# Reordering the side jobs of a decode layer's backward pass, with two small loads moved to the sync queue

## The chip, the cores and the metric

The kernel runs on one core of a Trainium2 chip. The time is device microseconds (us) of one execution; the median of three runs of the kernel before is 818.56 us, the runs lie between 818.16 and 818.86. One execution was profiled; what is read from its profile is set against that execution's own time, 818.39 us.

The core has five engines that run their own instruction streams in order: PE (matmul; its weight loads are listed as PEld), DVE (vector), ACT (scalar), POOL (GpSimd) and SP (sync). SP and POOL are used here above all to issue DMAs. The core's 16 DMA engines move the bytes.

## The reference

One decode step (one token, width D = 448) of a layer, forward and backward. In short:

```
h   = x  + Attention(layernorm(x))        # 16 query heads, 8 key/value heads, head width 256
h2  = h  + FFN(layernorm(h))              # (n @ w_gate) * (n @ w_up) @ w_down, width 1792
```

Attention looks only at the last W = 4096 of the 32768 cached positions. The outputs are h2 and the gradients of a loss with respect to x, k_cache, v_cache, wq, wo, w_gate, w_up and w_down, given grad_out, all in bf16. The two cache gradients have the caches' full shape, 8 x 32768 x 256 each: they are zero except in the window. Of these zeros 16 pieces (8 heads, two tensors) of 14.3 MB each have to be written, 234.9 MB in all. The nonzero windows are another 16 pieces of 2 MB.

## The kernel before

**Two DMA queues.** `FILL` is the sync queue (SP issues), `IO` the GpSimd queue (POOL issues). The sync queue carries only the 16 zero fills (L58), from one tile `zeros` of 128 x 8192 that DVE clears at the very start (L54). They are independent of all else. At most eight are outstanding: the ninth waits for the first to land, and so on. Everything else goes through the GpSimd queue in program order: inputs, windows of K and V, weights, and all other outputs.

**Start.** POOL first issues the two 0.9 KB rows x and grad_out (L88, L90), then Wq (L92, 3.5 MB), K and V windows (L75) and w_down (L97). Each row is needed by DVE for the first layernorm, after the clearing of `zeros`.

**Forward.** For each of the eight heads g: `scores`, `softmax`, `moments` (L266 to L329). Then wo (L376), the second layernorm, w_gate and w_up, and the gradients through the FFN (L423) to dh (L432), doT (L435), dq (L453 to L460).

**Backward.** A loop over g = 0..7 (stages). Each stage has 64 transposes of a V window on PE (L554), copied out of PSUM by ACT and DVE in turn (`evac`, L210 and L212); products dp (L559); some small work on DVE (L565 to L576); 32 matmuls `d_ps` (L588) whose results ACT and DVE copy to a staging slot; and two DMAs of 2 MB each to the cache gradients (L593). V windows of heads 5 to 7 are loaded again into slots that stages 1 to 3 have freed.

**Side jobs.** After each stage the list `side[g]` is run. Its jobs are
- `outer` (L472 to L477): one or two outer products' worth of rows of a weight gradient, made on DVE (L476) in one of two staging buffers in `Mt`, and one DMA on the GpSimd queue (L477). A buffer is free again when its DMA has landed. o6, o7: w_gate, w_up; o5: wo; o8: w_down; o4: wq.
- `ffn_out` (L490 to L501): loads w_down a second time into `Rt` (L492), 14 + 28 matmuls (L497, L159), and writes h2.
- `dxn_part` (L507 to L511): loads a part of Wq a second time into `Rt` (L508; 4 of 7 blocks, then 3), and reduces it against dq on DVE (L510).
- `dx_out`: the backward of the first layernorm (L194 to L203) and the output dx (L519).

`Rt` is one tile: w_up and the row `bc2[1]` that the o7 jobs read lie in it, then w_down, then the parts of Wq, so these follow each other. A scheduler orders the instructions of each engine; it moves ready work ahead of the program's order, so a job need not run where the program text has it.

Of the kernel before, what the change touches and what calls it, by code (L numbers as in the profile page):

```python
# [7 lines left out]
bf16 = mybir.dt.bfloat16  # L8
# [5 lines left out]
D = 448  # L14
# [14 lines left out]
HQ = H * Dh // 2  # L29
HF = F // 2  # L30
# [10 lines left out]
def kernel(  # L41
# [4 lines left out]
    FILL = nc.sync  # L46
    IO = nc.gpsimd

    const = ctx.enter_context(tc.tile_pool(name="const", bufs=1))
    small = ctx.enter_context(tc.tile_pool(name="small", bufs=2))  # L50
    ps = ctx.enter_context(tc.tile_pool(name="ps", bufs=1, space=bass.MemoryType.PSUM))

    zeros = const.tile([128, ZW], bf16)
    V_.memset(zeros[:], 0.0)  # L54
    for g in range(G):
# [27 lines left out]
    def flat_rows(w):  # L83
        return w.rearrange("a b -> (a b)").rearrange("(p x) -> p x", p=128)


    x_bf = const.tile([1, D], bf16, tag="rowa", name="x_bf")
    IO.dma_start(out=x_bf[:], in_=A_x.rearrange("a b d -> (a b) d"))  # L88
    go_bf = const.tile([1, D], bf16, tag="rowb", name="go_bf")
    IO.dma_start(out=go_bf[:], in_=grad_out.rearrange("a b d -> (a b) d"))  # L90
    wq_sb = S[:, 1:3, :].rearrange("p a b -> p (a b)")[:, 0:NI * HQ]
    IO.dma_start(out=wq_sb, in_=flat_rows(A_wq))  # L92
    load_K(0)
# [58 lines left out]
    def half_to_row(dst, z, bcast, first=True):  # L152

        d3 = dst.rearrange("o (m r) -> o m r", r=NI)
        n = 0
        for i in range(NI):
            for s in range(2):
                lt = z[:, i:i + 1].to_broadcast([128, 128]) if bcast else z[:, i:i + 1]
                P_.matmul(d3[:, :, (7 * s + i) // 2], lhsT=lt, rhs=ident_f[:, s::2],  # L159
                          start=(first and n == 0), stop=(n == 2 * NI - 1), skip_group_check=True)  # L160
                n += 1
# [6 lines left out]
    def layernorm(X, tag):  # L168
        s1 = small.tile([128, 1], f32, tag="ln_s")
        V_.reduce_sum(out=s1[:], in_=X, axis=AX)  # L170
        nm = small.tile([128, 1], f32, tag="ln_nm")
        V_.tensor_scalar(out=nm[:], in0=total(s1[:], 1)[:], scalar1=-1.0 / (2 * D), scalar2=None, op0=ALU.mult)
        xc = small.tile([128, NI], f32, tag="ln_xc")
        V_.tensor_scalar(out=xc[:], in0=X, scalar1=nm[:, 0:1], scalar2=None, op0=ALU.add)
        sq = small.tile([128, NI], f32, tag="ln_sq")
        s2 = small.tile([128, 1], f32, tag="ln_s2")
        V_.tensor_tensor_reduce(out=sq[:], in0=xc[:], in1=xc[:], scale=1.0, scalar=0.0, op0=ALU.mult, op1=ALU.add, accum_out=s2[:])
        rstd = const.tile([128, 1], f32, tag=tag + "rstd")
        S_.activation(out=rstd[:], in_=total(s2[:], 1)[:], func=ACT.Sqrt, bias=eps_t[:, 0:1], scale=1.0 / (2 * D))
        V_.reciprocal(out=rstd[:], in_=rstd[:])  # L180
        xh = const.tile([128, NI], f32, tag=tag + "xh")
        V_.tensor_scalar(out=xh[:], in0=xc[:], scalar1=rstd[:, 0:1], scalar2=None, op0=ALU.mult)
        xb = const.tile([128, NI], bf16, tag=tag + "xb")
        V_.tensor_copy(out=xb[:], in_=xh[:])
        xf = const.tile([128, NI], f32, tag=tag + "xf")
        V_.tensor_copy(out=xf[:], in_=xb[:])
        xx = const.tile([128, NI, 2], bf16, tag=tag + "xx")
        V_.tensor_tensor(out=xx[:], in0=xf[:].unsqueeze(2).to_broadcast([128, NI, 2]), in1=msk[:], op=ALU.mult)
        return rstd, xh, xf, xx
# [30 lines left out]
    rstd1, xh1, xf1, xx1 = layernorm(xX[:], "ln1")  # L220
# [21 lines left out]
    oT_f = const.tile([128, 32], f32)  # L242
    oT_bf = const.tile([128, 32], bf16)
    kbar = const.tile([128, 32], f32)
    dh2_bc = const.tile([128, D], bf16)
# [96 lines left out]
    bc2 = [S[:, 7, NI * HF:NI * HF + F].rearrange("p (i c) -> p i c", i=2), Rt[:, NI * HF:NI * HF + F].rearrange("p (i c) -> p i c", i=2)]  # L342
# [43 lines left out]
    rstd2, xh2, xf2, xx2 = layernorm(hX[:], "ln2")  # L386
# [44 lines left out]
    dh_bc = const.tile([128, D], bf16)  # L431
# [30 lines left out]
    dq_bc = late[:, 0:2 * HQ].rearrange("p (i c) -> p i c", i=2)  # L462
# [4 lines left out]
    def stage_buf():  # L467
        k = 1 + st_ctr[0] % 2
        st_ctr[0] += 1
        return late[:, k * 4096:(k + 1) * 4096]  # L470

    def outer(dst, n0, n1, src, scal, width):  # L472

        sb = stage_buf()[:, 0:(n1 - n0) * width].rearrange("p (n c) -> p n c", c=width)
        for n in range(n0, n1):
            V_.tensor_scalar(out=sb[:, n - n0, :], in0=src(n), scalar1=scal[:, n:n + 1], scalar2=None, op0=ALU.mult)  # L476
        IO.dma_start(out=dst[:, n0:n1, :], in_=sb)  # L477

    o4 = flat_rows(out_4).rearrange("p (i c) -> p i c", i=NI)
    o5 = out_5.rearrange("(b p) n -> p b n", p=128)  # L480
    o6 = flat_rows(out_6).rearrange("p (i c) -> p i c", i=NI)
    o7 = flat_rows(out_7).rearrange("p (i c) -> p i c", i=NI)
    o8 = out_8.rearrange("(c p) n -> p c n", p=128)

    hh = const.tile([128, FC], f32)
# [4 lines left out]
    def ffn_out():  # L490
        wd1 = Rt[:, 0:FC * D].rearrange("p (c n) -> p c n", n=D)
        IO.dma_start(out=wd1, in_=B_w_down.rearrange("(c p) n -> p c n", p=128))  # L492
        hX2 = small.tile([128, NI], f32, tag="hX2")
        V_.tensor_scalar(out=hX2[:], in0=hX[:], scalar1=0.5, scalar2=None, op0=ALU.mult)
        t = ps.tile([1, D], f32, tag="tmp", bufs=1)
        for c in range(FC):
            P_.matmul(t[:], lhsT=hh_bf[:, c:c + 1], rhs=wd1[:, c, :], start=(c == 0), stop=False, skip_group_check=True)  # L497
        half_to_row(t[:], hX2[:], False, first=False)
        h2 = const.tile([1, D], bf16, tag="rowb", name="h2")
        V_.tensor_copy(out=h2[:], in_=t[:])  # L500
        IO.dma_start(out=out_0.rearrange("a b d -> (a b) d"), in_=h2[:])  # L501

    Pq = const.tile([128, NI], f32)
    wq2 = Rt[:, 0:4 * HQ].rearrange("p (i c) -> p i c", c=HQ)
    wq_d = flat_rows(A_wq).rearrange("p (i c) -> p i c", i=NI)

    def dxn_part(i0, i1):  # L507
        IO.dma_start(out=wq2[:, 0:i1 - i0, :], in_=wq_d[:, i0:i1, :])  # L508
        for i in range(i0, i1):
            V_.tensor_tensor_reduce(out=wq2[:, i - i0, :], in0=wq2[:, i - i0, :], in1=dq_bc[:, i % 2, :], scale=1.0, scalar=0.0,  # L510
                                    op0=ALU.mult, op1=ALU.add, accum_out=Pq[:, i:i + 1])  # L511

    def dx_out():
# [4 lines left out]
        V_.tensor_copy(out=dx[:], in_=t[:])  # L518
        IO.dma_start(out=out_1.rearrange("a b d -> (a b) d"), in_=dx[:])  # L519

    side = {
        0: [lambda: outer(o6, 0, 4, lambda i: bc2[0][:, i % 2, :], xf2, HF), lambda: outer(o6, 4, 7, lambda i: bc2[0][:, i % 2, :], xf2, HF),
            lambda: outer(o7, 0, 4, lambda i: bc2[1][:, i % 2, :], xf2, HF), lambda: outer(o7, 4, 7, lambda i: bc2[1][:, i % 2, :], xf2, HF)],
        1: [ffn_out] + [lambda b=b: outer(o5, b, b + 8, lambda n: dh_bc[:], oT_f, D) for b in (0, 8)],
        2: [lambda b=b: outer(o5, b, b + 8, lambda n: dh_bc[:], oT_f, D) for b in (16, 24)],
        3: [lambda b=b: outer(o8, b, b + 7, lambda n: dh2_bc[:], hh, D) for b in (0, 7)],
        4: [lambda: dxn_part(0, 4)],
        5: [lambda: dxn_part(4, 7), dx_out],
        6: [lambda i=i: outer(o4, i, min(i + 2, 7), lambda n: dq_bc[:, n % 2, :], xf1, HQ) for i in (0, 2)],
        7: [lambda i=i: outer(o4, i, min(i + 2, 7), lambda n: dq_bc[:, n % 2, :], xf1, HQ) for i in (4, 6)],  # L530
    }


    STG = [5, 6, 7, 0]
# [3 lines left out]
    rowb = late[:, 14336:16384].rearrange("p (k a c) -> p k a c", k=2, a=8)  # L538
# [7 lines left out]
    for g in range(G):  # L546
# [36 lines left out]
        for c in range(T // 2):  # L583
            d_ps = bps.tile([128, 2, 2, Dh], f32, tag="d2", bufs=2)
            for i in range(2):
                t = 2 * c + i
                k, a = t // 8, t % 8
# [38 lines left out]
```

## Time and profile before

| What | Value |
|---|---|
| Median of three runs | 818.56 us |
| The profiled execution: time / span of its instructions | 818.39 / 816.6 us |
| PE, DVE, ACT, POOL busy | 61%, 46%, 20%, 5% of the span |
| Bytes moved by DMA | 338.66 MB: 234.88 MB on the sync queue, 103.00 MB on the GpSimd queue, the rest instruction loads |
| Mean DMA rate over the span | 415 GB/s |
| Granted PE clock | 0.85 to 0.91 of full in the first 200 us, 0.50 to 0.53 from 400 us on |

How to read it: the profile divides the span into slices and gives for each engine the busy share, for the DMA engines the mean busy share of all 16 and the bytes moved. A stretch in which all 16 are busy reads 1.00 or 1.01. A wait is listed with the instruction that waited, what released it, the total in us, how often, and the longest one. For a DMA the time from its issue to its landing is given.

### The profile page before, as it was taken

How to read it: one execution, taken by the hardware profiler on the slowest of the kernel's cores; microseconds unless marked ns; L12 is line 12 of the kernel's file. 1: busy time of each engine (PE TensorE's matmuls, PEld its weight loads, DVE VectorE, ACT ScalarE, POOL GpSimd, SP SyncE). 2: the span in 40 equal slices, each digit the busy share in tenths (PEclk: the TensorE clock that was granted, in tenths of full speed). 3: DMA queues.
4: the chain of work that ended last, by engine and by line, in shares of the span. 5: the costliest groups of instructions: out<-in, count | busy, mean ns of one | idle time of the engine just before them, and what ended most of it. 6: DMA issues, size and time to landing. Idle time of an engine off the chain costs nothing.

```text
span 816.6 us, 12117 instructions
## 1 busy us (share of the span) xinstructions
PE 497.6 (61%) x4947; PEld 300.9 (37%) x4991; DVE 376.8 (46%) x1149; ACT 164.9 (20%) x261; POOL 41.7 (5%) x77
## 2 busy tenths in 40 slices
PE   3558869999574946062993468799378940001770
PEld 3545646666343523031981332345124410001110
DVE  4127847667461643028732354565255440404550
ACT  0220201221101000000011233355244420000440
POOL 4000000000000001000000000010010000000000
PEclk9959888999695969565555556555555555555555
DMA  8999999999999999999999999999999999999985
GB/s 322 431 424 429 427 429 426 429 427 426 432 423 426 424 420 418 427 429 432 423 430 427 417 413 426 428 402 429 419 404 426 423 428 400 424 415 432 431 355 237
DMA packets 24632, 338.66 MB, mean 415 GB/s; under 512 B 1312, under 2 KB 1376, under 8 KB 4736
## 3 DMA queue, kind: packets, MB, share of 16 engines
q1 hardware_dynamic: 14592, 234.88, 68.2%
q0 software_dynamic: 9984, 103.00, 30.2%
q8 instruction: 39, 0.64, 0.3%
q14 instruction: 17, 0.14, 0.0%
HBM read 57.28 MB, written 280.59 MB: 414 GB/s over the span
## 4 chain that ended last, share of the span: by engine, by line
issue 50%; DMA 22%; PE 14%; another core or an unknown queue 4%; DVE 4%; POOL 2%; ACT 1%; POOLq 0%; DVEq 0%; ACTq 0%
DMA out_dram<-Mt 9%; DMA out_dram<-S 5%; DMA S<-in_A_wo_dram 4%; PE dq_ps L453 3%; PE d_ps L588 3%; PE tr L554 2%; DMA S<-in_A_v_cache_dram 2%; DMA S<-in_A_wq_dram 2%; PE MT L322 2%; DVE Rt L423 1%; DVE Rt L510 1%; POOL S L75 1%; PE dh_ps L159 1%; DVE S L212 1%
## 5 line engine op out<-in xcount | busy, mean ns | idle before, releaser
L322 PE MATMUL MT<-Rt,S 128*128 128x512 bf16 x468 | 146.7, 391 | 22.5 <-DMA S<-in_A_v_cache_dram 19.8
L588 PE MATMUL d_ps<-R,Mt 32*128 32x512 bf16 x256 | 121.1, 605 | 58.6 <-DVE S L212 57.9
L318 DVE TENSOR_SCALAR Rt<-S,pf 128x256 bf16<-128x256 bf16 x512 | 118.0, 282 | 31.6 <-PE acc L329 16.5
L212 DVE CAST S<-d_ps 128x512 bf16<-128x512 f32 x128 | 87.1, 689 | 63.4 <-ACT S L210 55.6
L210 ACT CAST S<-d_ps 128x512 bf16<-128x512 f32 x128 | 74.9, 586 | 127.7 <-PE d_ps L588 127.7
L266 PE MATMUL tr<-ident_bf,S 128*128 128x128 bf16 x512 | 51.5, 264 | 43.4 <-DMA S<-in_A_k_cache_dram 40.1
L325 PEld LDWEIGHTS <-S 128*128 128x128 bf16 x512 | 50.1, 99 | 62.9 <-issue 7.2
L554 PE MATMUL tr<-ident_bf,S 128*128 128x128 bf16 x512 | 67.6, 304 | 0.7 <-ACT Mt L210 0.7
L588 PEld LDWEIGHTS <-Mt 32*128 32x128 bf16 x256 | 22.8, 113 | 112.8 <-issue 110.8
L329 PE MATMUL acc<-ones_bf,Rt 128*128 128x1 bf16 x1024 | 62.0, 164 | 0.0
L554 PEld LDWEIGHTS <-S 128*128 128x128 bf16 x512 | 48.4, 136 | 24.4 <-issue 24.4
L266 PEld LDWEIGHTS <-S 128*128 128x128 bf16 x512 | 40.5, 120 | 41.9 <-DMA S<-in_A_k_cache_dram 40.6
L325 PE MATMUL acc<-pT_all,S 128*128 128x2 bf16 x512 | 49.3, 166 | 2.6 <-issue 0.9
L165 PE MATMUL t<-st,ones_f 128*128 128x2 f32 x4 | 1.2, 364 | 79.6 <-DVE st L196 79.6
L210 ACT COPY Rt<-tr 128x1024 bf16<-128x1024 bf16 x32 | 32.4, 1012 | 85.1 <-PE tr L266 84.6
L210 ACT COPY Mt<-tr 128x1024 bf16<-128x1024 bf16 x32 | 32.4, 1014 | 60.8 <-PE tr L554 34.3
L329 PEld LDWEIGHTS <-Rt 128*128 128x128 bf16 x1024 | 44.5, 96 | 0.0
L212 DVE COPY Rt<-tr 128x1024 bf16<-128x1024 bf16 x32 | 22.1, 689 | 47.5 <-PE tr L266 46.2
L322 PEld LDWEIGHTS <-S 128*128 128x128 bf16 x512 | 32.2, 97 | 22.3 <-DMA S<-in_A_v_cache_dram 20.0
L331 ACT COPY Mt<-MT 128x512 f32<-128x512 f32 x8 | 4.7, 586 | 165.1 <-remote 73.8
L510 DVE CUSTOM_DVE_ANT_0 Rt<-Rt,Mt 128x2048 bf16<-128x2048 bf16 x7 | 15.6, 2289 | 48.3 <-DMA Rt<-in_A_wq_dram 48.3
L212 DVE COPY Mt<-tr 128x1024 bf16<-128x1024 bf16 x32 | 22.0, 686 | 22.9 <-PE tr L554 15.5
(184 smaller groups left out, 463.5 us busy)
## 6 DMA issues: line engine op xcount, KB each, us to landing
out_dram<-zeros SPq DMA_DIRECT2D x16, 14336.0 KB, 155.7
out_dram<-S POOLq DMA_DIRECT2D x16, 2048.0 KB, 31.0
S<-in_A_v_cache_dram POOLq DMA_DIRECT2D x11, 2048.0 KB, 35.6
S<-in_A_k_cache_dram POOLq DMA_DIRECT2D x8, 2048.0 KB, 27.9
out_dram<-Mt POOLq DMA_DIRECT2D x6, 896.0 KB, 18.2
S<-in_A_wq_dram POOLq DMA_DIRECT2D x1, 3584.0 KB, 15.3
S<-in_A_wo_dram POOLq DMA_DIRECT2D x2, 1792.0 KB, 35.6
out_dram<-Mt POOLq DMA_DIRECT2D x3, 1024.0 KB, 32.5
```

The lines of the kernel that those rows point to most:

```text
L75: IO.dma_start(out=dst, in_=cache[0, g, Sk - W:, :].rearrange("(p t) d -> p t d", t=T))
L210: S_.copy(out=out, in_=in_)
L212: V_.tensor_copy(out=out, in_=in_)
L266: P_.transpose(tr[:, i, dh, :], Xw[:, 4 * q + i, dh * 128:(dh + 1) * 128], ident_bf[:])
L318: V_.tensor_scalar(out=pk[:, i, h, :], in0=K[:, t, :], scalar1=pf[:, t, h:h + 1], scalar2=None, op0=ALU.mult)
L322: P_.matmul(MT[:, hf, :], lhsT=Vv[:, t, hf * 128:(hf + 1) * 128], rhs=pk[:, i, :, :].rearrange("p h d -> p (h d)"), start=(t == 0), stop=( ...
L325: P_.matmul(acc[:, 2 * hf:2 * hf + 2], lhsT=Vv[:, t, hf * 128:(hf + 1) * 128], rhs=pT_all[:, g, t, :], start=(t == 0 and hf == 0), stop=(t ...
L329: P_.matmul(acc[:, 4 + 2 * h + dk:5 + 2 * h + dk], lhsT=pk[:, i, h, dk * 128:(dk + 1) * 128], rhs=ones_bf[:, 0:1], start=False, stop=(t == ...
L453: P_.matmul(dq_ps[:, 2 * h + dk:2 * h + dk + 1], lhsT=Mt[:, h // 2, hf, c0:c0 + 128], rhs=doT_f[:, 2 * h + hf:2 * h + hf + 1], start=(hf = ...
L510: V_.tensor_tensor_reduce(out=wq2[:, i - i0, :], in0=wq2[:, i - i0, :], in1=dq_bc[:, i % 2, :], scale=1.0, scalar=0.0, op0=ALU.mult, op1=A ...
L554: P_.transpose(tr[:, i, dh, :], Vw[g][:, 4 * q + i, dh * 128:(dh + 1) * 128], ident_bf[:])
L588: P_.matmul(d_ps[:, i, :, :].rearrange("p w d -> p (w d)"), lhsT=rows[32 * k:32 * k + 32, a, :], rhs=R[32 * k:32 * k + 32, :], start=True, ...
```

## The change

The loads of x and grad_out are issued first of all by SP on the sync queue, ahead of the fills. `dxn_part` no longer loads; a new `dxn_load` does. The second load of w_down with `ffn_out`, the two o7 jobs, and the load of the first part of Wq stand ahead of the stage loop. The first reduction and the second load of Wq come with stage 0, the second reduction and dx with stage 1; o5, o8 and o4 follow in stages 2 to 6, and stage 7 has no side job.

```diff
+    x_bf = const.tile([1, D], bf16, tag="rowa", name="x_bf")
+    FILL.dma_start(out=x_bf[:], in_=A_x.rearrange("a b d -> (a b) d"))
+    go_bf = const.tile([1, D], bf16, tag="rowb", name="go_bf")
+    FILL.dma_start(out=go_bf[:], in_=grad_out.rearrange("a b d -> (a b) d"))
     zeros = const.tile([128, ZW], bf16)
     V_.memset(zeros[:], 0.0)
...
-    x_bf = const.tile([1, D], bf16, tag="rowa", name="x_bf")
-    IO.dma_start(out=x_bf[:], in_=A_x.rearrange("a b d -> (a b) d"))
-    go_bf = const.tile([1, D], bf16, tag="rowb", name="go_bf")
-    IO.dma_start(out=go_bf[:], in_=grad_out.rearrange("a b d -> (a b) d"))
     wq_sb = S[:, 1:3, :].rearrange("p a b -> p (a b)")[:, 0:NI * HQ]
...
+    def dxn_load(i0, i1):
+        IO.dma_start(out=wq2[:, 0:i1 - i0, :], in_=wq_d[:, i0:i1, :])
+
     def dxn_part(i0, i1):
-        IO.dma_start(out=wq2[:, 0:i1 - i0, :], in_=wq_d[:, i0:i1, :])
         for i in range(i0, i1):
...
     side = {
-        0: [o6 rows 0-4, o6 rows 4-7, o7 rows 0-4, o7 rows 4-7],
-        1: [ffn_out, o5 rows 0-8, o5 rows 8-16],
-        2: [o5 rows 16-24, o5 rows 24-32],
-        3: [o8 rows 0-7, o8 rows 7-14],
-        4: [lambda: dxn_part(0, 4)],
-        5: [lambda: dxn_part(4, 7), dx_out],
-        6: [o4 rows 0-2, o4 rows 2-4],
-        7: [o4 rows 4-6, o4 row 6],
+        0: [o67_job(0, 0, 4), o67_job(0, 4, 7), lambda: dxn_part(0, 4), lambda: dxn_load(4, 7)],
+        1: [lambda: dxn_part(4, 7), dx_out],
+        2: [o5_job(0), o5_job(8)],
+        3: [o5_job(16), o5_job(24)],
+        4: [lambda b=b: outer(o8, b, b + 7, lambda n: dh2_bc[:], hh, D) for b in (0, 7)],
+        5: [o4_job(0), o4_job(2)],
+        6: [o4_job(4), o4_job(6)],
+        7: [],
     }
+    ffn_out()
+    o67_job(1, 0, 4)()
+    o67_job(1, 4, 7)()
+    dxn_load(0, 4)
```

(The removed lists of jobs are written out in words here; `o4_job`, `o5_job` and `o67_job` are the same calls of `outer` as before under a name.) In the changed program POOL issues, from the end of the FFN's backward on: w_down, two outputs of weight gradients, h2, one output, Wq blocks 0 to 3, two outputs, the V window, Wq blocks 4 to 6, and only then the two windows of stage 0.

More of the change, by code (lines that the diff above doesn't have):

```diff
@@ L519, in dx_out, with o4_job, o5_job, o67_job @@
         IO.dma_start(out=out_1.rearrange("a b d -> (a b) d"), in_=dx[:])
-    side = {
[L522 to L526, printed above, removed]
-        4: [lambda: dxn_part(0, 4)],
-        5: [lambda: dxn_part(4, 7), dx_out],
-        6: [lambda i=i: outer(o4, i, min(i + 2, 7), lambda n: dq_bc[:, n % 2, :], xf1, HQ) for i in (0, 2)],
-        7: [lambda i=i: outer(o4, i, min(i + 2, 7), lambda n: dq_bc[:, n % 2, :], xf1, HQ) for i in (4, 6)],
-    }
+    def o4_job(i):
+        return lambda: outer(o4, i, min(i + 2, 7), lambda n: dq_bc[:, n % 2, :], xf1, HQ)
+    def o5_job(b):
+        return lambda: outer(o5, b, b + 8, lambda n: dh_bc[:], oT_f, D)
+    def o67_job(w, i0, i1):
+        return lambda: outer((o6, o7)[w], i0, i1, lambda i: bc2[w][:, i % 2, :], xf2, HF)
+    side = {
+        0: [o67_job(0, 0, 4), o67_job(0, 4, 7), lambda: dxn_part(0, 4), lambda: dxn_load(4, 7)],
[6 more added lines that the diff above has]
+        7: [],
+    }
+    ffn_out()
+    o67_job(1, 0, 4)()
+    o67_job(1, 4, 7)()
+    dxn_load(0, 4)
     STG = [5, 6, 7, 0]
```

## The prediction

> **What bounds the kernel now.** I read the page's slices first, then the stretches of the end, then the DMA records of the last 27 us, then the waits. The DMA row of the page and its rates:
>
> ```profile
> DMA  8999999999999999999999999999999999999985
> GB/s 322 431 424 429 427 429 426 429 427 426 432 423 426 424 420 418 427 429 432 423 430 427 417 413 426 428 402 429 419 404 426 423 428 400 424 415 432 431 355 237
> ```
>
> From the second slice to the 38th the 16 DMA engines are never free, while PE, DVE and ACT often are. The bytes, then, and not the chain of computation, set the pace, and the only places where time can be won are the first and the last 20 us. I asked for both in stretches (columns: length, busy us of the engines, granted PE clock, DMA share, GB/s):
>
> ```profile
> 0.00:2.40 2.40, 0.00 (x0) 0.00 (x0) 0.73 (x1) 1.28 (x1) 1.30 (x6) 1.00 0.00 0
> 2.40:7.00 4.60, 1.26 (x6) 1.26 (x7) 4.60 (x13) 0.00 (x0) 4.55 (x11) 1.00 0.84 287
> 20.00:777.00 757.00, 475.01 (x4883) 290.45 (x4928) 355.10 (x1085) 153.41 (x242) 30.94 (x50) 0.65 1.01 424
> 777.00:789.00 12.00, 9.11 (x21) 2.14 (x20) 6.85 (x10) 5.66 (x10) 1.09 (x2) 0.50 0.98 420
> 789.00:798.00 9.00, 6.00 (x13) 1.17 (x11) 5.37 (x8) 4.28 (x8) 0.27 (x1) 0.50 0.50 215
> 798.00:808.00 10.00, 0.00 (x0) 0.00 (x0) 0.16 (x1) 0.00 (x0) 0.79 (x2) 0.50 0.95 401
> 808.00:814.00 6.00, 0.00 (x0) 0.00 (x0) 0.00 (x0) 0.00 (x0) 0.00 (x0) 0.50 0.23 96
> ```
>
> For 757 us the share is 1.01 at 424 GB/s, which is 26.5 GB/s for each of 16 engines. From 789 to 798 half is idle: stage 7 is not ready, its outputs are issued at 797.73 and 798.45 us. This looks like time to be won, and it is the trap of this profile. The DMA view of the window 790 to 817 (slices of 0.675 us) shows why:
>
> ```profile
> DMA  9754343333222999999999999995211110100000
> GB/s 388 340 218 194 170 194 146 146 146 170 121 97 121 388 413 437 510 437 413 388 413 485 388 413 413 437 485 243 121 49 73 49 49 24 49 0 0 0 0 0
> q1 hardware_dynamic: 46, 0.66, 5.7%
> ```
>
> In the slices from 792 to 798 the rate is still 97 to 194 GB/s: four to seven engines work on, on 0.66 MB of zeros (q1 is the sync queue) that are left to them. After 809 the rate is 24 to 73 GB/s, which is one to three engines. So the engines do not finish together. The packet records of the trace give the end of the last fill per engine: ten between 777.6 and 784.9 us, the others at 792.0, 792.5, 797.1, 798.0, 803.0 and 805.0. Followed back from the last packet of the kernel (ends 814.2), that last engine's packets stand end to end at least back to 760 us; before 777 no engine had a gap, as the share shows. **The slowest DMA engine is busy from its first packet at 3.7 us to 814.2 us. Its work is the time**; what the other fifteen leave idle before the last outputs is not on the path. One engine trails in earlier fills too (in the eighth to tenth fill the last completion comes 9 to 10 us after the second-to-last).
>
> What lies around it: 2.4 us from 814.2 to the span's end 816.6 (landing 0.45 us, closing barriers), and 1.79 us from the span to 818.39.
>
> **The change part by part.**
>
> *The two rows.* POOL's first issues are:
>
> ```profile
> 1.31 0.62 POOL L88 DMA_DIRECT2D x_bf<-in_A_x_dram  x1 [0.85 <-POOLq L610]
> 1.93 0.50 POOL L90 DMA_DIRECT2D go_bf<-in_grad_out_dram  x1
> 2.42 0.55 POOL L92 DMA_DIRECT2D S<-in_A_wq_dram  x1
> ```
>
> Without the first two, Wq is issued at 1.31 instead of 2.42: 1.11 us earlier, and with it its first packet (3.66 before, 1.24 us after the issue; 2.55 then). Wq, two K windows, one V window and w_down, 11.5 MB or 27 us at 424 GB/s, stand in that queue, so all engines, the slowest too, start 1.11 us earlier and stay fed. Gain 1.11 us. On SP the rows take two issues, at most about 2 x 0.62 us by the shortest fill issue, from 1.67 to 2.9 us; the first fill waits for DVE's clearing of the zeros until 5.17 anyhow, which hides them. Without that cover the fills would come 1.2 us late, and the 27 us of loads would still keep the engines busy. The rows are wanted by DVE at 5.35, behind the clearing; landing took 1.7 to 1.8 us, which is 3.6 to 4.7. A fill still waits for the one eight before it, since the rows take two of the eight semaphores first and are long done. Bounds of this edit: 0 to 1.11; I take 1.11, because the issue rows show it directly.
>
> *The side jobs.* No byte, no matmul and no DVE instruction is added or removed; 338.66 MB stay. What moves is the chain. Its worst stalls were here:
>
> ```profile
> DVE Mt L476 <- DMA out_dram<-Mt: 75.3, 11, 10.8
> DVE Rt L510 <- DMA Rt<-in_A_wq_dram: 48.3, 2, 24.9
> PE t L165 <- DVE st L196: 79.6, 2, 67.4
> ```
>
> DVE stood 48.3 us before the two reductions (675.7 to 700.6 and 709.6 to 732.9), and behind them waited everything that DVE does for stages 6 and 7; PE waited up to 67.4 us. The stages' second outputs were issued at 504.4, 537.8, 572.0, 605.4, 642.4 and 676.0: 34.3 us a stage, PE at half clock being its limit. Then came 778.8 and 798.5. In the changed order the two reductions (7 x 2.29 = 16.0 us of DVE) stand within stages 0 and 1, and each still waits for its load: the second load is issued only when the first reduction is done, and after 0.9 MB of output and 2 MB of V. POOL issues stage 0's windows behind it. Stage 0 then comes at 504.4 + 16.0 + w, where w is the wait for the two loads, and stage 7 at 520.4 + 7 x 34.3 + w = 760.5 + w. The row gives w between 0 and 48.3. I take 25: the first load has the head's DVE work before it (it should be nearly there), the second is the 23 to 25 us row again. That is 785 for the last outputs instead of 798.5, bounds 760 to 809. The w_down load with its 42 matmuls on PE is hidden: it landed 25.8 us after its issue at 384.8, at 410.5, while PE was on the dq matmuls (L453) until 419.7. Uncovered, the 42 matmuls would cost some 5 us, out of w's slack. The o7 jobs come first because their tile must be free for Wq; they use the same two buffers, and the 75.3 us of buffer waits move with the jobs and are on the chain only.
>
> Does an earlier stage 7 help? It fills the half-idle stretch of fifteen engines. The slowest engine had no gap there; it works through the same fills and the same 16 packets of the last windows in another order. So nothing is gained, as long as its share of the last windows is queued before its other work runs out: 16 packets of 0.61 us are 9.8 us, so by about 803 in the old clock, 802 in the new. Worth of the side jobs: 0. Its bounds are the rivals below.
>
> The lag grew unevenly: 16.2 us between the first and the last engine at the sixth to eighth fill (302 to 402 us), 26 at the eleventh (509 to 535), 27 at the end. By these rows it depends on what is mixed with the fills when, and could change by some us (rival C). [...] The trace shows one engine last each time, but does not name it.
>
> **Sum.** 818.39 - 1.11 - 0 = 817.3 for the profiled execution, whose time is 0.17 below the median; against 818.56 that is **817.4 us**, 0.14% faster.
>
> **The rivals.**
>
> *A. The tail is filled.* If the trailing engines lag because of how the work falls late in the kernel, and not by their whole work, all 16 finish together. From 789 on 9 x 215 + 10 x 401 + 6 x 96 = 6.5 MB moved, or 15.4 us at 424 GB/s: 804.4, less 1.1, plus 2.4 and 1.8 is 807.5. For it: half of the engines' time in 789 to 798 and three quarters in 808 to 814 is idle. Against: the end-to-end packets of the last engine. A partial win, with a smaller lag, lies between 807.5 and 817.
>
> *B. The wait at the head (slower).* If both Wq loads are waited for in full and the new first stages collect buffer waits besides, w exceeds 42 us and the last outputs are issued after 802. From there each us costs one, since the other engines are then out of work. At w = 48.3 they come at 809 instead of 798.5; from issue to the span's end it is then 1.24 us to the first packet, 9.8 for the 16 packets and 2.4, 13.4 in all: 809 + 13.4 + 1.8 = 824. For it: the wait has moved and not gone. Against: 17 us of slack at my value of w.
>
> *C. The slowest engine falls further behind.* Its lag behind the median engine was 3.3 us at the second fill and 23 at the last, so contention costs it as much as it does; another mix of transfers could change that by some 3 us either way. Upwards this gives 819 to 822, and downwards 814.
>
> *D. The rows bring nothing,* because the first packets are held by something else: 818.6.
>
> **Numbers.** What a measurement of this kernel can tell from no change is about 0.2%, 1.6 us. Forecast (the slowest engine's work, C's small swings in it): 0.62, own range 814 to 820; of it 0.24 faster, 0.34 same, 0.04 slower. A: 0.17, faster. B: 0.08, slower. C upwards and D: 0.13, of it 0.09 slower and 0.04 same. Together faster 0.41, same 0.38, slower 0.21. The range 811 to 821.5 leaves out most of A (0.12) and the far ends of B and C (0.06).
>
> **What would show it.** The first Wq packet about 1.1 us earlier. Last outputs issued around 785; L512 (the old L510) waiting 25 us or so near 500 instead of 48 near 700. Then a tail of the other shape: 16 engines busy to about 788 or a little later, then ten or more idle together, and one to three engines at 25 to 75 GB/s of zeros until about 813; the wait that ends the kernel is on a fill or on late windows, not on stage 7. Wrong it would be if the DMA share stays at 1.0 to within 3 us of the end (A), or if the last outputs come after 802 (B).

## The result, and the profile after

The changed kernel takes 816.49 us (median of ten runs, 816.18 to 817.20) against 818.58 for the kernel before on the same chip: 0.9961 of it, 95% interval 0.9944 to 0.9978. The forecast was 817.4, faster by less than it came out. The stated range, 811 to 821.5, holds the time of no change as well, so it is the packet records and the experiments that test the mechanism. The two medians alone differ by 2.09 us or 0.26%; the ratio lies lower because three of the ten runs of before took 821 to 823 us and none of after did, a spread that also stands in the experiments below (before up to 824.30, the rows alone up to 822.83, the jobs alone up to 817.49) and whose cause is not known, since none of the long executions was profiled. The profiled execution of after took 816.48 us, its span is 814.7 (before 818.39 and 816.6).

The page's DMA row and rates of after:

```profile
DMA  8999999999999999999999999999999999999993
GB/s 344 430 423 427 430 428 429 425 428 426 430 417 426 415 424 420 428 429 431 426 427 429 409 415 421 431 423 422 404 430 425 425 413 423 421 425 427 424 427 170
```

The slice before the last is full now (427 GB/s instead of 355) and the last one emptier (170 instead of 237): the same bytes, earlier. The stretches of after (length, busy us of PE, PEld, DVE, ACT, POOL, clock, DMA share, GB/s):

```profile
2.40:7.00 4.60, 1.33 (x7) 1.33 (x7) 4.59 (x13) 0.00 (x0) 4.57 (x13) 1.00 1.08 386
20.00:777.00 757.00, 496.63 (x4959) 294.60 (x4959) 364.97 (x1102) 163.42 (x259) 33.21 (x54) 0.65 1.01 424
789.00:798.00 9.00, 0.00 (x0) 0.00 (x0) 0.00 (x0) 0.00 (x0) 0.00 (x0) 0.50 0.97 415
798.00:808.00 10.00, 0.00 (x0) 0.00 (x0) 0.00 (x0) 0.00 (x0) 0.00 (x0) 0.50 0.42 182
808.00:814.00 6.00, 0.00 (x0) 0.00 (x0) 0.00 (x0) 0.00 (x0) 0.00 (x0) 0.50 0.05 22
```

The hole at 789 to 798 is filled (0.97 for 0.50), and what the fifteen faster engines gained there they now idle away after 798 (0.42 for 0.95, 0.05 for 0.23). A share of 0.05 is not even one engine of 16 for the whole stretch. The DMA view of after from 790 to 817, the same window as shown of before:

```profile
DMA  9999999999889965455322111101000000000000
GB/s 413 461 413 510 413 413 437 437 388 413 364 364 437 388 291 218 194 218 218 170 97 97 73 73 73 73 24 49 24 24 24 24 24 24 0 0 0 0 0 0
```

From 807.7 on the rate is 24 GB/s: one engine works through zeros alone. The packet records, which give each packet's start, end and queue, say the same: the last fill ends on fifteen engines between 796.9 and 807.7 us and on the sixteenth at 813.1.

At the head, the DMA view of the first 8 us (slices of 0.2 us), first of before, then of after:

```profile
DMA  0000000000000000009989430039973499933349
```

```profile
DMA  0000000000000995730003997009933009933049
```

The first 9 stands in the 19th slice before and in the 14th after: the first large packet starts at 3.66 and at 2.66 us. The issues that stand behind this, and the last two outputs, in the timeline of POOL in after:

```profile
1.29 0.67 POOL L92 DMA_DIRECT2D S<-in_A_wq_dram  x1 [0.83 <-POOLq L624]
...
761.19 0.53 POOL L607 DMA_DIRECT2D out_dram<-S  x1 [16.40 <-ACT S L210]
761.91 0.53 POOL L607 DMA_DIRECT2D out_dram<-S  x1 [0.19 <-issue]
```

Wq is issued 1.13 us earlier, the last outputs 36.5 us earlier (before: 797.73 and 798.45). The waits of after that answer to those shown of before:

```profile
DVE Mt L476 <- DMA out_dram<-Mt: 72.4, 10, 11.9
DVE Rt L512 <- DMA Rt<-in_A_wq_dram: 25.9, 2, 21.1
PE t L165 <- DVE st L196: 12.3, 1, 12.3
```

The reductions wait 25.9 us for their Wq parts instead of 48.3, PE 12.3 us for the layernorm's backward instead of 79.6, and the buffer waits are as they were. All this is off the path.

Put together by the packet records: first large packet 1.00 us earlier; from it to the last packet 810.51 us before and 810.43 after; from the last packet to the span's end 2.43 us before and 1.62 after. That is -1.00 - 0.08 - 0.81 = -1.9 us, the whole difference of the spans. The stretch after the last packet is called the closing below.

### The profile page after: what moved, and what is told of

Its sections match the earlier page's. It is cut to its first block, busy times and chain, and to the rows that moved or that the text cites. A ratio compares the mean times of both kernels' runs of the same rounds, so it can differ in the third digit from the quotient of the medians.

```text
span 814.7 us, 12155 instructions
## 1 busy us (share of the span) xinstructions
PE 504.1 (62%) x4991; PEld 301.7 (37%) x4991; DVE 374.4 (46%) x1149; ACT 165.0 (20%) x261; POOL 40.4 (5%) x75
## 4 chain that ended last, share of the span: by engine, by line
issue 59%; DMA 17%; PE 11%; DVE 4%; POOL 3%; ACT 1%; POOLq 0%; DVEq 0%
DMA S<-in_A_wo_dram 4%; DMA Rt<-in_A_wq_dram 4%; DMA out_dram<-Mt 3%; PE dq_ps L453 3%; DMA S<-in_A_k_cache_dram 3%; DMA S<-in_A_v_cache_dram 2%; PE MT L322 2%; POOL out_dram L477 1%; POOL S L79 1%; DVE Rt L423 1%; POOL out_dram L607 1%; PE dh_ps L159 1%; PE d_ps L602 1%; PE tr L568 1%; PE t L413 1%
## 5 line engine op out<-in xcount | busy, mean ns | idle before, releaser
L602 PE MATMUL d_ps<-R,Mt 32*128 32x512 bf16 x256 | 124.4, 612 | 94.4 <-DVE S L212 93.6
L322 PE MATMUL MT<-Rt,S 128*128 128x512 bf16 x512 | 156.8, 391 | 21.1 <-DMA S<-in_A_v_cache_dram 19.9
L266 PE MATMUL tr<-ident_bf,S 128*128 128x128 bf16 x512 | 52.5, 267 | 44.5 <-DMA S<-in_A_k_cache_dram 41.2
L568 PE MATMUL tr<-ident_bf,S 128*128 128x128 bf16 x512 | 68.8, 304 | 3.5 <-ACT Mt L210 3.5
L573 PEld LDWEIGHTS <-Mt 128*128 128x128 bf16 x512 | 19.9, 108 | 36.7 <-DVE Mt L212 13.7
L573 PE MATMUL dp<-doT,Mt 128*128 128x2 bf16 x512 | 22.6, 168 | 12.3 <-DVE Mt L212 10.5
## 6 DMA issues: line engine op xcount, KB each, us to landing
S<-in_A_wq_dram POOLq DMA_DIRECT2D x1, 3584.0 KB, 14.7
```

Of the source, the lines that this page charges most:

```text
L266: P_.transpose(tr[:, i, dh, :], Xw[:, 4 * q + i, dh * 128:(dh + 1) * 128], ident_bf[:])
L322: P_.matmul(MT[:, hf, :], lhsT=Vv[:, t, hf * 128:(hf + 1) * 128], rhs=pk[:, i, :, :].rearrange("p h d -> p (h d)"), start=(t == 0), stop=( ...
L568: P_.transpose(tr[:, i, dh, :], Vw[g][:, 4 * q + i, dh * 128:(dh + 1) * 128], ident_bf[:])
L573: P_.matmul(dp[:, 4 * q + i, :], lhsT=xt[:, i, dh, :], rhs=doT[:, 4 * g + dh:4 * g + dh + 3:2], start=(dh == 0), stop=(dh == 1))
L602: P_.matmul(d_ps[:, i, :, :].rearrange("p w d -> p (w d)"), lhsT=rows[32 * k:32 * k + 32, a, :], rhs=R[32 * k:32 * k + 32, :], start=True, ...
```

## The experiments

**Theory:** the slowest DMA engine is busy from its first packet to the end, so an earlier start counts one for one, and the chain of computation not at all up to a threshold near 802 us. **Rivals:** the earlier chain itself brings the gain, or the rows bring nothing.

### The rows alone

The kernel before, with only the two row loads moved to the sync queue.

```diff
+    FILL.dma_start(out=x_bf[:], in_=A_x.rearrange("a b d -> (a b) d"))
+    FILL.dma_start(out=go_bf[:], in_=grad_out.rearrange("a b d -> (a b) d"))
     zeros = const.tile([128, ZW], bf16)
...
-    IO.dma_start(out=x_bf[:], in_=A_x.rearrange("a b d -> (a b) d"))
-    IO.dma_start(out=go_bf[:], in_=grad_out.rearrange("a b d -> (a b) d"))
```

> The kernel before with only the two rows moved to the sync queue; the side jobs in their old order. Theory (the slowest DMA engine's whole work sets the end; the rows let it start earlier): first Wq packet at 2.7 us instead of 3.7, last packet about 1.0 us earlier (813.1), the closing 2.4 us as before, so 817.5 against 818.5. Rival (the new order of the side jobs made the gain by filling the idle tail): 818.5, no change.

Measured: 817.39 us, 0.9976 of before (0.9956 to 0.9997). First packet 2.67, last packet 813.04, closing 2.42. The last outputs stay at 797.78 and 798.51. The earlier start alone gives 1.1 us of the span (816.6 to 815.5), with a chain as late as before.

### The jobs alone

The changed kernel with the rows back on the GpSimd queue (the same lines the other way round).

> The changed kernel with the two rows back on the GpSimd queue: only the side jobs are reordered. Theory: the first packet stays at 3.7 and the last at about 814.2 us; only the closing after the last packet shrinks from 2.4 to 1.6 us, since no window output ends the kernel: 817.7 against 818.5. Rival (the tail is filled): the last packet moves to 813 or earlier, 816.5 to 817.

Measured: 817.20 us, 0.9966 (0.9951 to 0.9980). First packet 3.69, last packet 814.17, as in before to 0.01 us, though the last outputs come at 761.95 and 762.67. The chain did not move the last packet's end; the gain of 1.2 us in the span is all in the closing (1.26 instead of 2.43).

### The last stage late, by 19 and by 59 us

The changed kernel, with the DVE product of stage 7 made 18 and 50 times; nothing else differs.

```diff
-        V_.tensor_tensor(out=rows, in0=r_ps[:]...
+        for _ in range(18 if g == 7 else 1):
+            V_.tensor_tensor(out=rows, in0=r_ps[:]...
```

> The changed kernel, with one DVE operation of stage 7 (the 128 x 1024 product, 1.23 us) done 18 times instead of once, which makes the chain of computation about 20 us later: last outputs near 782 instead of 762. Theory: the end does not see it as long as the last outputs are issued before about 802: 816.5, within 0.5. Rival (the chain's end counts): 830 to 838.

Measured: 816.47 us, 0.9956 (0.9940 to 0.9972), last outputs at 780.53 and 781.26: 19 us more of chain cost nothing.

> The changed kernel, with the same DVE operation of stage 7 done 50 times instead of once: the last outputs then are issued near 820 instead of 762, after the point (about 802) from which the theory lets them set the end. Theory: last issue 820 + 1.2 + 9.9 for 4 MB + 2.4 closing + 1.8 = 835 (832 to 838), so that the first 40 us of delay cost nothing and the rest costs one for one. Rival (the chain always counts): 816.5 + 58 = 874.

Measured: 834.23 us, 1.0184 (1.0150 to 1.0217). The DMA view of the window 788 to 833 (slices of 1.1 us) shows the case past the threshold:

```profile
DMA  8853222100000000000000000000097999969900
GB/s 379 350 248 146 102 102 87 73 29 29 29 36 29 0 0 0 0 0 0 0 0 0 0 0 0 0 0 0 0 408 291 466 466 466 451 277 437 466 0 0
```

One engine ends at about 803, then all are idle until the last outputs are issued at 819.93 and 820.66; from 820.66 it is 12.4 us to the span's end at 833.1, where the prediction had 13.4. Against after's span of 814.7 that puts the threshold at 814.7 - 12.4 = 802.3 us. By it 18.4 us of the delay lie past the threshold; the median is 17.7 us above that of after.

### Wq first, on the sync queue

The changed kernel with Wq's first load at the head of the sync queue, and the rows on the scalar queue.

```diff
...
+    FILL.dma_start(out=wq_sb, in_=A_wq.rearrange("a b -> (a b)").rearrange("(p x) -> p x", p=128))
-    FILL.dma_start(out=x_bf[:], ...)
+    nc.scalar.dma_start(out=x_bf[:], ...)
...
-    IO.dma_start(out=wq_sb, in_=flat_rows(A_wq))
```

> The changed kernel with the first load of Wq issued on the sync queue ahead of the fills, and the two rows on the scalar queue. In the changed kernel the first packet of a row on the sync queue stands at 1.6 us, that of Wq on the GpSimd queue at 2.7. Theory (the slowest engine's end is its start plus its work): first Wq packet near 1.7, last packet 1.0 earlier, 815.5. Rival (the start does not matter, or the GpSimd queue is not ready any earlier to keep the engines fed): 816.5.

Measured: 816.27 us, 0.9962 (0.9946 to 0.9978). The first packet comes 0.89 us earlier (1.77), the last 0.55 (812.54). The median is nearer to the rival's 816.5 than to the 815.5 expected (the profiled execution took 815.86): 0.34 us of the earlier start are lost in the engine's work, which varies by that much between kernels:

| Kernel | First packet | Last packet | Between | Closing | Span |
|---|---|---|---|---|---|
| before | 3.66 | 814.17 | 810.51 | 2.43 | 816.6 |
| rows alone | 2.67 | 813.04 | 810.38 | 2.42 | 815.5 |
| jobs alone | 3.69 | 814.17 | 810.48 | 1.26 | 815.4 |
| after | 2.66 | 813.09 | 810.43 | 1.62 | 814.7 |
| after, stage 7 19 us late | 2.66 | 813.37 | 810.71 | 1.67 | 815.0 |
| Wq on the sync queue | 1.77 | 812.54 | 810.77 | 1.54 | 814.1 |

By its median this is the fastest version, but 0.2 us are less than the two kernels' runs scatter.

### Why does one engine end last?

Four kernels, each measured in one execution, that move the same zeros (16 fills of 14,336 KB, 14.7 MB each) and leave out the rest; the first on the sync queue alone.

> Only the 16 zero fills, on the sync queue; everything else is left out and no other output is written. How far the slowest engine ends behind the median one with nothing mixed in. If the lag comes from the mix with other transfers or from the GpSimd queue's traffic: under 3 us, and about 234.9 MB / 429 GB/s + 9 + 2 = 558 us. If one engine is slow by itself: a lag of 15 us or more.

Measured: 559.3 us; all 16 engines end every fill within 0.2 us of each other (the last at 556.2 to 556.3).

> Only the 16 zero fills, on the GpSimd queue. [...] If the mix of transfers makes the lag: under 3 us, and 558 us as on the sync queue.

The edit is `FILL = nc.gpsimd`. Measured: 564.36 us; the last fill ends at 557.1 to 557.3 on eight engines and at 560.8 to 560.9 on the other eight. The 3.6 us between the halves for 235 MB do not account for the 23 of the kernel before (805.0 against a median of 782.3), where that queue carries 103 MB.

> Only the 16 zero fills on the sync queue, and beside them 4700 small matmuls on PE, as many PE instructions as the whole kernel has, so that the instruction loads (39 of 16 KB in the kernel before) are there and no data traffic on the GpSimd queue; everything else is left out. If the slowest engine lags because it loads the instructions as well: a lag of some 10 to 30 us behind the median engine at the last fill. If the mix of data transfers makes the lag: under 2 us, 559 us as with the fills alone.

```diff
+    for n in range(4700):
+        P_.matmul(t[:], lhsT=one[:], rhs=one[:, 0:2], start=(n == 0), stop=(n == 4699), skip_group_check=True)
```

Measured: 575.08 us. The DMA view from 550 us to the end (slices of 0.58 us):

```profile
DMA  9999999999554532000000000000000000000000
GB/s 394 450 450 422 450 450 450 450 422 450 253 253 197 225 169 113 28 28 28 28 28 28 28 28 28 28 28 28 28 28 28 28 28 28 28 28 28 0 0 0
```

Seven engines end by 556.6, eight by 559.5, and one goes on alone at 28 GB/s until 572.2. The 36 loads of 16 KB of instructions are all that was added to the DMA engines. They start between 12.1 and 254.4 us, and the lag follows them: the last engine ends 0.3 us behind the next one at the first fill (44 us), 13.4 at the seventh (266 us), and stays at 13.4 to 12.7 from there to the end.

> Only the 16 zero fills on the sync queue, and beside them 24 loads and 24 stores of 2 MB windows on the GpSimd queue (100.7 MB, the kernel before has 103.0 there); no computation, and so hardly any instruction loads; everything else is left out. If the mix of data transfers makes the lag: 10 us or more behind the median engine at the last fill. If the instruction loads make it: some 2 us, as the GpSimd queue alone shows (3.6 us for 235 MB). Time by bytes: 335.6 MB at 427 GB/s, 786 us, plus 9.

```diff
+    for n in range(24):
+        IO.dma_start(out=dst, in_=cache[0, g, Sk - W:, :]...)
+        IO.dma_start(out=o[0, g, Sk - W:, :]..., in_=dst)
```

Measured: 814.38 us with no computation at all. The DMA view from 780 us to the end (slices of 0.81 us):

```profile
DMA  9999989967423222222211111111111111011000
GB/s 467 426 386 487 426 345 487 446 284 304 203 122 162 101 101 122 101 101 122 101 81 81 81 81 81 81 81 81 81 81 81 81 81 61 41 61 61 20 0 0
```

Eleven engines end at 786.9 to 789.2; the slowest ones at 791, 797, 807, 810 and 811: four engines' worth of rate and less, for 20 us. The GpSimd queue's transfers end at 517 us; the fill that ends then has 24 us between its first and its last engine (1 us at the first fill), and the last fill has 24 still. So there are two causes, each of which makes a lag by itself: instruction loads held up one engine (12.7 us at the end), and loads and stores on the GpSimd queue beside the fills held up several (24 us between the first and the last). Whether they would do so on another queue was not tried. How the two add up in the kernel is not shown, nor which engines they are: the records name none.

### Relieving the slow engine by hand

The changed kernel with the last fill cut up, meant to give the engines unequal shares: in a first kernel 640 rows on 128 partitions, 240 on 120 and 16 on 16, in a second six rows for each of 128 partitions and 8 partitions of 16 rows. That 120 partitions give the engines unequal shares is not shown by any run.

```diff
-            FILL.dma_start(out=reg, in_=zeros[:].unsqueeze(1).to_broadcast([128, NZ, ZW]))
+            if g < G - 1 or o is out_2:
...
+            else:
...
+                for p0, r0, n in ((128, 0, 5), (120, 640, 2), (16, 880, 1)):
...
+                    FILL.dma_start(out=part, in_=zeros[0:p0, :].unsqueeze(1).to_broadcast([p0, n, ZW]))
```

> The changed kernel, whose last fill is cut in three: 640 rows of 16 KB by 128 partitions, 240 rows by 120 partitions and 16 rows by 16 partitions. [...] Rival (the sum of bytes over all engines counts): 816.5, no change.

Measured: 826.20 us, 1.0070 (1.0044 to 1.0096), 9.7 us more than after and so not the 816.5 of no change. From 780 us on the 16 KB packets of the sync queue took 772 ns on average, and 53 of the 402 took 1.15 to 1.3 us, about twice the 611 to 620 of most others.

> The changed kernel, with the last row set (128 rows of 16 KB) of its last output fill handed over as 8 partitions of 16 rows, at the same row pitch, instead of 128 partitions of one row; the output is the same. The changed kernel stands at 816.49 us, last packet 813.1. Question: is the DMA engine that ends last in the kernel always the same one, and can it be relieved by hand. [...] If the transfer is spread over all engines regardless of its partitions, the time stays at 816.5 with 0.5 either way.

```diff
...
+            else:
+                FILL.dma_start(out=reg[:, 0:NZ - 1, :], in_=zeros[:].unsqueeze(1).to_broadcast([128, NZ - 1, ZW]))
+                FILL.dma_start(out=reg[:, NZ - 1, :].rearrange("(a b) f -> a b f", a=8), in_=zeros[0:8, :].unsqueeze(1).to_broadcast([8, 16, ZW]))
```

Measured: 840.58 us, 1.0260 (1.0213 to 1.0308), 24.1 us more than after; the time did not stay at 816.5. The stretch 808 to 830 of it:

```profile
808.00:830.00 22.00, 0.00 (x0) 0.00 (x0) 0.00 (x0) 0.00 (x0) 0.00 (x0) 0.50 0.46 52
```

Seven to eight engines are busy (0.46 of 16) and move 52 GB/s together; the 8 partitions were not spread over all 16. To see what makes the packets long, the fills alone were run in several forms:

```diff
+            if form == "N": pieces = [(reg, 128, NZ)]
+            elif form == "A": pieces = [(reg[:, r:r + 1, :], 128, 1) for r in range(NZ)]
...
+            for dst, p0, k in pieces:
+                FILL.dma_start(out=dst, in_=zeros[0:p0, :].unsqueeze(1).to_broadcast([p0, k, ZW]))
```

> The fills alone on the sync queue (nothing else is computed or moved, so the other outputs stay undefined), 234.9 MB, but in several forms one after the other, to see why the packets of the tail took longer in the two runs that cut the last fill: 3 fills as they are (128 partitions, 7 rows of 16 KB each, one behind the other); 3 as seven transfers of 128 rows at 112 KB pitch (form A); 3 as six rows for each of 128 partitions and then 8 partitions of 16 rows at 112 KB pitch (form B, that of the run with 8 partitions); 3 as the same 8 partitions, the rows contiguous (form C); 3 as 640 rows on 128, 240 on 120 and 16 on 16 partitions (form D, that of the run with 120 partitions); one as it is. A packet of 16 KB took 611 ns in the plain fills alone. If it is the row pitch: A and B above 1000 ns, C and D near 611. If it is eight engines that each read one partition again and again: B and C above 1000 ns on the short transfer, A and D near 611. If the form is innocent: all within 611 to 640 ns, and the whole takes 559 us plus at most 5 us for engines that wait for nothing.

The stretches of this kernel (length, DVE, POOL, clock, DMA share, GB/s), the first in form A, the others where only short transfers of forms B and C are left:

```profile
120.00:200.00 80.00, 0.00 (x0) 0.00 (x0) 1.00 1.01 427
320.00:330.00 10.00, 0.00 (x0) 0.00 (x0) 1.00 0.51 52
460.00:480.00 20.00, 0.00 (x0) 0.00 (x0) 1.00 0.49 51
```

Form A runs at full rate (617 ns a packet): the pitch is not it. With 8 partitions as the source eight engines move 52 GB/s, 2,532 ns a packet, whatever the pitch: that is it. Whether it is that each engine reads one partition again and again, or that the eight partitions are neighbours, these forms do not separate. Form D ran beside what was left of C and can't be read by itself, so the first cut (120 partitions) is not settled. Which engine is the slow one stays open too; the two cut fills cost more than they could have told.

## Why the prediction was right, and where not

- **The bound** held. Between first and last packet the six kernels of the table lie within 0.4 us, with the last outputs anywhere from 754 to 798 us. Those 0.4 us are also how closely "one for one" is shown: the last packet came 1.13 us earlier for the rows' 0.99, and 0.55 for the 0.89 of Wq on the sync queue.
- **The rows**, -1.11: the first packet came 1.00 us earlier; the issue gave 1.13, but the first packet followed it by 1.37 us instead of 1.24. SP issued the rows at 0.76 and 1.12 us, where 1.67 to 2.9 was forecast, and the first fill at 5.18, behind the clearing as before. Rival D is refuted by the rows alone.
- **The side jobs**, worth 0: right for the packets (814.17 with and without them), wrong in the term that was taken as fixed, "2.4 us from 814.2 to the span's end". With the jobs reordered it is 1.3 to 1.7 us. This is the term that makes 816.5 of 817.4. The semaphore records show where it comes from. At the close GpSimd answers a barrier that Sync has signalled: in before at 815.86 us, 0.76 after Sync's signal at 815.10; in after at 813.98, 0.03 after it. In before and in all the runs here the answer comes 0.60 to 0.87 us after Sync where the last packet is one of the GpSimd queue (before, the rows alone, stage 7 59 us late, the fills on the GpSimd queue) and 0.03 us where it is one of the sync queue (all others). Two pairs of kernels differ in little else: with stage 7 59 us late it is 0.63, with 19 us 0.03; with the fills alone on the GpSimd queue 0.60, on the sync queue 0.03. So the late end of GpSimd's transfers is what lengthens the closing; what GpSimd does in that time is not shown.
- **Last outputs** at 785: came at 761.9. The wait itself was sized right (25.9 for 25). The step that failed is adding w and the reductions' 16 us in full, 41 together: the second output of stage 0 came at 519.0, 14.6 us after the 504.4 of before, so some 26 us lay beside other work; which part of the two it was is not separated. The stages then took 34.7 us each (34.3 forecast). The bounds 760 to 809 held it. The tail has the forecast shape, one engine alone until 813.1, but all engines were busy until about 798 and not 788.
- **The threshold** at 802: 802.3 by the run with 59 us more. Rival B is a true mechanism with 40 us to spare, where the forecast had 17.
- **Rival A** (the tail is filled): refuted, the jobs alone left the last packet where it was. The idle time of fifteen engines only moved from 789-798 to 798-814.
- **Rival C**, 3 us either way: the mechanism exists (the mix of transfers alone made a lag of 22 us), but its swing from one order of jobs to the other was 0.1 us and 0.4 over all six kernels. The engine that ends last has its own work and does not care when the others idle. What made a lag by itself was the GpSimd queue's loads and stores beside the fills (24 us between the first and the last engine) and the instruction loads (12.7 us behind the next engine), but not that queue alone: with only the fills on it the engines ended 3.6 us apart, eight and eight.

## What to carry to other kernels

Where all DMA engines look busy, look at each one's last packet: here the one that ended last (its last fill at 805.0 us, the median engine's at 782.3) set the time, and the idle share of the others near the end was nothing to be won by an earlier chain (last packet at 814.17 with the outputs 36 us earlier). What counts then is when the first large transfer is issued (two small loads ahead of it on the same queue cost 1.0 us here) and what the engines have to close after the last packet (1.26 to 2.43 us here), which is a term to be worked out and not to be carried over. A chain that ended before its threshold cost nothing (816.47 us with stage 7 19 us later), and the one run past it paid about one us for one us (17.7 us for 18.4); work out the threshold first.

## What was not expected of the hardware

- 36 instruction loads of 16 KB, 0.59 MB beside 235, put one DMA engine 12.7 us behind the next one. By an estimate, at the 26.5 GB/s of one engine (424 GB/s over 16 in the kernel before), these bytes would be 22 us if all fell on one engine, so their share on the slow one could explain it; the records do not tell which engine carried them.
- Fills on the sync queue beside loads and stores on the GpSimd queue let four engines fall 8 to 22 us behind the median one, without any computation; the lag stayed when the fills went on alone.
- The kernels whose last packet belongs to the GpSimd queue close 0.6 to 0.8 us later after Sync's signal than those whose last packet belongs to the sync queue.
- Eight engines that read from eight neighbouring partitions get 51 to 52 GB/s in all, 6.5 each, a quarter of the 26.7 GB/s that each has in form A of the fills (427 GB/s over 16).
